# The first expert's order of work: token blocks in halves, the first product's bank copied when its scale is known, weight preparation, maxima and two gate rounds moved

## The chip, the cores and the metric

The kernel runs on one core of a Trainium2 chip. The metric is the device time of one execution in microseconds (us). TensorE (PE) multiplies matrices into PSUM, ACT (ScalarE), DVE (VectorE) and POOL (GpSimd) do the rest, SP issues the DMAs. Each engine works through its own queue in order and waits at an instruction until what it needs is there.

## The reference

Three stages, each feeding the next. Attention over 2 batches, 8 heads, 576 positions and head dimension 64, with a learned bias by relative position. A first mixture: `h = max(x@w1, x@w2, x@w3)`, `x = h@w_out`, on 1152 tokens (512 features, 768 hidden). A second mixture of eight experts:

```python
logits = x @ w_gate
P = np.exp(logits - logits.max())
for _ in range(8):
    P /= P.sum(1, keepdims=True) + 1e-09
    P /= P.sum(0, keepdims=True) + 1e-09
    P *= N / E
for e in range(E):
    h = np.maximum(x @ w1[e], 0.0)
    out += P[:, e:e + 1] * (h @ w2[e])
```

with x of 1152 x 512, `w1[e]` of 512 x 1024 and `w2[e]` of 1024 x 512.

## The kernel before, in words

The change lies at the end of the first mixture and the start of the second. `tc.manual_schedule()` is on: every engine's queue holds its instructions in the order in which the Python code emits them, so the lists of small functions below are the schedule. Numbers are kept as a high and a low half-precision part (`h` and `l` in the names), and each product is three matmuls: high by high, low by high, high by low. A high part is an ACT copy, a low part a subtraction on DVE or GpSimd.

**The last stage of the first mixture** (loop from L1066, matmuls on L1073) makes x in sixteen output tiles, k = 0 to 15, each of 18 matmuls: four feature blocks d for the token groups 0, 2, 1, 3 in this order. After the matmuls of a tile come its eviction (`x_ev`: ACT scales it into `x2f`, DVE takes its maximum into `xm`), and then the steps that `sched[k]` lists. These are:

- `x_top`, `x_scale`: the scale of x.
- `pf0`, `pf1` (from `prep_f`, L930): the weights w1 of the first two halves of the first expert; six steps each: `scale` (ACT into tile `wf`, of which there is one), `s13` and `s24` (two DVE sums each), `a_split` (ACT high, GpSimd low, 768 columns), `hi_s` (ACT, 1024 columns), `lo_s` (GpSimd, 1024 columns).
- `bs0`, `bs1`: the token blocks B11 and B21 for the first and second half of the tokens of a batch (ACT high, GpSimd low).
- `xs0`, and for the second half `last` (both from `x_steps`, L970): the other five token blocks. `t1`, `tb`, `t2`, `t4` are DVE subtractions, `h2` to `h6` high parts on ACT, `l2` to `l6` low parts (`l2` and `g6` on GpSimd, the others on DVE).
- `p2(i)` (`prep_2`, L1025): a quarter of a w2 block: two ACT operations, one GpSimd low part, and the load of a later quarter on SP.
- `pk`, `peak_join`, `peak_send`, `peak_get`, `peak_all`: maxima of raw weights on DVE, sent through memory to all partitions (`SC` is that of w2 of the second block, `S2` of later ones); `b_top` and `b_all` do the same for `SB` on TensorE.

**The second mixture** (loop from L1325) has 32 calls `up(n)` and 16 calls `down(h)`: up(0), up(1), up(2), down(0), up(3), up(4), down(1), up(5) and so on. `up(n)` forms four quarter results with seven products in Strassen's manner (Winograd's form) in three PSUM banks x, z and y; `prod` issues a product of 12 matmuls, `snap` copies a bank on ACT with the scale c, `join` adds a bank on DVE, `relu_hi` (ACT) and `relu_lo` (DVE) write the two parts of h. The first, fourth and sixth products all go into bank x: the fourth can begin only when `snap` has read the first. c comes from the largest |x| (`m_top` and `m_spread`, one small TensorE operation each, then a few DVE operations), and that needs the last tile's maximum. `then(seg)` runs what `between` (and `extra`) put at seven places of an `up`.

`down(h)` runs nine token tiles t of 12 matmuls each into two PSUM banks; each is added into `acc` (ACT for h = 0, DVE after that), and the lists `todo[t]` prepare the next weights. The gate's rounds are spread over this time: `cols` is a small matmul that sums P over the tokens, followed by four DVE operations; `rows` is four DVE operations. In down(0) `rows` stand at t = 0, 2, 4, 6 and `cols` at t = 2, 4, 6; up(4) and up(5) hold two rounds each; up(6) has the last `cols`.

Of the kernel before, what the change touches and what calls it, by code (L numbers as in the profile page):

```python
# [15 lines left out]
ALU = mybir.AluOpType  # L16
# [38 lines left out]
def make_body(stop=None):  # L55
    def body(tc, a):
# [21 lines left out]
        with ctx, tc.manual_schedule():  # L78
# [770 lines left out]
            with ExitStack() as mctx:  # L849
# [120 lines left out]
                def x_steps(s):  # L970
# [6 lines left out]
                    return {"t1": sub(t1, bl(0, 1), bl(0, 0)), "t2": sub(t2, bl(1, 1), t1), "tb": sub(tb, bl(1, 1), bl(0, 1)),  # L977
# [72 lines left out]
                def b_all():  # L1050
# [6 lines left out]
                sched = {0: [x_top], 1: [x_scale], 2: [pf0[0]], 3: pf0[1:3] + [pk(1, 1, 0)], 4: [pf0[3], pk(1, 1, 1)],  # L1057
                         5: [pf0[4], pf0[5], pk(0, 2, 0), pk(0, 2, 1)],
                         6: [bs0[0], pk(0, 2, 2), pk(0, 2, 3), lambda: peak_join(*SB)], 7: [b_top, bs0[1], pf1[0]],
                         8: [b_all] + xs_("t1", "tb", "h2", "l2"), 9: xs_("h3", "h5", "t2") + pf1[1:3], 10: xs_("l3", "l5", "h4") + pf1[3:4],  # L1060
                         11: xs_("l4", "t4") + pf1[4:6] + [pk(1, 2, 0)], 12: xs_("h6", "g6") + [bs1[0], pk(1, 2, 1), pk(1, 2, 2)],
                         13: [bs1[1], p2(0), pk(1, 2, 3), lambda: peak_join(*SC)], 14: [p2(1), lambda: peak_send(SC[0])],
                         15: [end(n) for n in ("t2", "h2", "l2", "h3")]}
                sched[14] += [lambda: last.update(x_steps(1)), end("t1")]
# [31 lines left out]
            with ExitStack() as ectx:  # L1096
# [80 lines left out]
                def m_spread():  # L1177
# [8 lines left out]
                between = {(0, 0): [m_top, end("h4"), end("l3")],  # L1186
                           (0, 1): [m_spread, end("l4"), end("tb"), end("h5"), end("l5")], (0, 2): [end("t4")],
                           (0, 3): [end("h6"), end("l6")], (0, 6): [p2(2)], (1, 5): [p2(3)],
                           (1, 6): [logits], (2, 1): [flip], (2, 2): [gate], (1, 2): [lambda: peak_get(SC[0])],
                           (2, 0): [lambda: peak_all(*SC)], (2, 6): []}  # L1190
# [11 lines left out]
                def up(n, extra):  # L1202
# [11 lines left out]
                    def prod(i, j, bank, start):  # L1214
# [5 lines left out]
                        for c in range(2):  # L1220
                            for ws, xs in ((whi, xth), (whi, xtl), (wlo, xth)):
# [4 lines left out]
                                k += 1  # L1226
                        return ps[bank][:, :, :SH]
# [23 lines left out]
                    then(0)  # L1251
                    z = prod(A12, B21, "z", True)
                    if n == 0:
                        then(1)
                        s1 = snap("s1", x)
# [5 lines left out]
                    if n > 0:  # L1261
                        relu_lo(0, 0, s1)
# [138 lines left out]
```

## Time and profile before

| | us |
|---|---|
| median of three runs | 1076.03 (1075.59 to 1076.33) |
| the profiled execution | 1074.92 |
| its span, first to last instruction | 1073.1 |
| PE busy | 1041.2 (97%) |
| DVE busy | 794.3 (74%) |
| ACT busy | 593.1 (55%) |
| POOL busy | 403.6 (38%) |

The granted clock of TensorE was 0.993 of full speed on average. Times in the rows are from the span's start. Matmuls overlap, and a matmul's end is modelled, so a TensorE that is busy all the time can still lose time; what it loses is read from the spacing of the starts and from the marks of idle time.

### The profile page before, as it was taken

How to read it: one execution, taken by the hardware profiler on the slowest of the kernel's cores; microseconds unless marked ns; L12 is line 12 of the kernel's file. 1: busy time of each engine (PE TensorE's matmuls, PEld its weight loads, DVE VectorE, ACT ScalarE, POOL GpSimd, SP SyncE). 2: the span in 40 equal slices, each digit the busy share in tenths (PEclk: the TensorE clock that was granted, in tenths of full speed). 3: DMA queues.
4: the chain of work that ended last, by engine and by line, in shares of the span. 5: the costliest groups of instructions: out<-in, count | busy, mean ns of one | idle time of the engine just before them, and what ended most of it. 6: DMA issues, size and time to landing. Idle time of an engine off the chain costs nothing.

```text
span 1073.1 us, 18471 instructions
## 1 busy us (share of the span) xinstructions
PE 1041.2 (97%) x7145; PEld 731.8 (68%) x7145; DVE 794.3 (74%) x1547; ACT 593.1 (55%) x1003; POOL 403.6 (38%) x285
## 2 busy tenths in 40 slices
PE   7779999999999899999999999999999999999998
PEld 3259988999999765564755746657566575664753
DVE  8999999799967776877667677566675666757543
ACT  7989988544425666544545444545445454544530
POOL 6996998122214424135132141331413314123120
PEclk8999999999999999999999999999999999999999
DMA  5878764244522012013021120221302203110002
GB/s 187 278 232 276 223 193 136 62 158 118 121 74 84 21 62 64 26 59 84 20 64 36 49 84 21 64 53 32 84 21 65 64 29 76 23 42 6 1 1 89
DMA packets 41063, 90.78 MB, mean 85 GB/s; under 512 B 8264, under 2 KB 11280, under 8 KB 40080
## 3 DMA queue, kind: packets, MB, share of 16 engines
q1 hardware_dynamic: 40832, 89.31, 28.3%
q8 instruction: 56, 0.92, 0.4%
q14 instruction: 31, 0.25, 0.1%
q10 hardware_dynamic: 144, 0.29, 0.1%
HBM read 75.50 MB, written 13.30 MB: 83 GB/s over the span
## 4 chain that ended last, share of the span: by engine, by line
PE 83%; DVE 9%; ACT 3%; POOL 2%; issue 2%; DMA 0%; DVEq 0%; ACTq 0%; POOLq 0%
PE d L1304 34%; PE x L1223 12%; PE m L658 10%; PE y L1223 8%; PE z L1223 8%; PE sc L482 3%; PE o L1073 2%; PE pv L608 2%; POOL s L356 2%; PE pt L556 2%; DVE ng L499 1%; PE p L381 1%; DVE ptl L570 1%; DVE hl L1244 1%; DVE s L1235 1%
## 5 line engine op out<-in xcount | busy, mean ns | idle before, releaser
L1304 PE MATMUL d<-w2h,hl 128*128 128x512 f16 x576 | 218.3, 379 | 0.2 <-DVE hl L1244 0.2
L1304 PE MATMUL d<-w2h,hh 128*128 128x512 f16 x576 | 218.3, 379 | 0.0
L1304 PE MATMUL d<-w2l,hh 128*128 128x512 f16 x576 | 218.3, 379 | 0.0
L1223 PEld LDWEIGHTS <-w1h 128*128 128x128 f16 x1792 | 175.0, 98 | 52.6 <-issue 5.7
L1304 PEld LDWEIGHTS <-hh 128*128 128x128 f16 x1152 | 112.6, 98 | 132.4 <-ACT hh L1239 0.4
L953 POOL TENSOR_TENSOR w1l<-wf,w1h 128x768 f16<-128x768 f32 x32 | 53.2, 1663 | 362.6 <-ACT w1h L952 289.4
L1318 DVE SCALAR_TENSOR_TENSOR acc<-d,kh,acc 128x512 f32<-128x512 f32 x126 | 94.3, 749 | 93.7 <-PE d L1304 93.6
L1239 ACT ACTIVATE hh<-s 128x576 f16<-128x576 f32 x128 | 87.3, 683 | 128.5 <-DVE s L1235 99.9
L1244 DVE SCALAR_TENSOR_TENSOR hl<-s,hh 128x576 f16<-128x576 f32 x128 | 99.2, 776 | 46.7 <-ACT hh L1239 44.2
L959 POOL TENSOR_TENSOR w1l<-wf,w1h 128x1024 f16<-128x1024 f32 x32 | 69.3, 2166 | 117.1 <-ACT w1h L956 117.1
L956 ACT ACTIVATE w1h<-wf 128x1024 f16<-128x1024 f32 x32 | 33.8, 1055 | 131.2 <-DVE wf L949 131.2
L1304 PEld LDWEIGHTS <-hl 128*128 128x128 f16 x576 | 56.4, 98 | 68.5 <-DVE hl L1244 0.7
L1223 PEld LDWEIGHTS <-w1l 128*128 128x128 f16 x896 | 87.7, 98 | 22.1
L1231 ACT ACTIVATE s<-x,cx 128x576 f32<-128x576 f32 x96 | 70.4, 733 | 28.5 <-PE x L1223 28.3
L1223 PE MATMUL x<-xth,w1h 128*128 128x288 f16 x384 | 78.4, 286 | 2.9 <-ACT s L1231 2.9
L1034 POOL TENSOR_TENSOR w2l<-w2r,w2h 128x512 f16<-128x512 f32 x64 | 74.0, 1178 | 17.5 <-ACT w2h L1033 17.5
L1223 PE MATMUL x<-xth,w1l 128*128 128x288 f16 x384 | 78.4, 286 | 0.0
L1223 PE MATMUL x<-xtl,w1h 128*128 128x288 f16 x384 | 78.4, 286 | 0.0
L1235 DVE SCALAR_TENSOR_TENSOR s<-z,cx,s 128x576 f32<-128x576 f32 x64 | 52.3, 818 | 31.3 <-PE z L1223 24.9
L658 PE MATMUL m<-xl,wh 128*128 128x384 f32 x216 | 72.5, 336 | 0.0
L658 PE MATMUL m<-xh,wh 128*128 128x384 f32 x216 | 72.4, 335 | 0.0
L658 PE MATMUL m<-xh,wl 128*128 128x384 f32 x216 | 72.4, 335 | 0.0
(225 smaller groups left out, 2332.7 us busy)
## 6 DMA issues: line engine op xcount, KB each, us to landing
wr<-in_moe_w SPq DMA_DIRECT2D x50, 512.0 KB, 3.6
w2r<-in_moe_w SPq DMA_DIRECT2D x64, 256.0 KB, 2.8
bias_f<-bo SPq DMA_DIRECT2D x36, 295.5 KB, 3.4
bias<-bias_f SPq DMA_DIRECT2D x32, 288.0 KB, 2.8
qk<-in_qk SPq DMA_DIRECT2D x7, 1152.0 KB, 6.9
wr<-in_moe_w_out SPq DMA_DIRECT2D x6, 512.0 KB, 5.3
vr<-in_v SPq DMA_DIRECT2D x8, 320.0 KB, 7.2
bias<-bias_f SPq DMA_DIRECT2D x16, 144.0 KB, 5.0
```

Of the source, the lines that this page charges most:

```text
L658: T.matmul(out=p[:, :TG], lhsT=ws[:, 128 * c:128 * c + 128], rhs=xs[:, c, TG * g:TG * g + TG], start=(c == 0 and n == 0), stop=(c == 3 and ...
L953: G.tensor_tensor(out=lo[:, 0:3], in0=t[:, 1:4], in1=hi[:, 0:3], op=ALU.subtract)
L956: A.activation(out=hi[:, 3:7], in_=t[:, 4:8], func=AF.Copy)
L959: G.tensor_tensor(out=lo[:, 3:7], in0=t[:, 4:8], in1=hi[:, 3:7], op=ALU.subtract)
L1034: G.tensor_tensor(out=lo, in0=r, in1=hi, op=ALU.subtract)
L1223: T.matmul(out=ps[bank][:, s, :SH], lhsT=ws[:, i, c, :], rhs=xs[:, j, c, s * SH:s * SH + SH], start=(start and k == 0), stop=(k == 5), **kw)
L1231: A.activation(out=t, in_=src, func=AF.Identity, scale=c)
L1235: V.scalar_tensor_tensor(out=out, in0=z, scalar=scale, in1=out, op0=ALU.mult, op1=ALU.add)
L1239: A.activation(out=o, in_=src, func=AF.Relu)
L1244: V.scalar_tensor_tensor(out=l, in0=src, scalar=0.0, in1=o, op0=ALU.max, op1=ALU.subtract)
L1304: T.matmul(out=pd, lhsT=hs[:, fh, 128 * t:128 * t + 128], rhs=ws, start=(k == 0), stop=(k == 11))
L1318: V.scalar_tensor_tensor(out=acc[:, t, :], in0=pd, scalar=kh[:, 1 + t:2 + t], in1=acc[:, t, :], op0=ALU.mult, op1=ALU.add)
```

## The change

It splits three steps of block B22 for the second half of the tokens by feature half (`t2a`, `t2b` and so on); reorders `sched`, so that the first token blocks come at k = 4 and 5, the second weight half at k = 6 to 8, the first two `p2` at k = 9 and 10, and the three maxima of `SC` leave k = 11 to 13; gives `prod` a place in the middle (`mid`), at which up(0) now runs `m_top`; puts the copy `s1` of up(0) directly behind `then(1)`, ahead of the copy `s5`, and the join behind `then(2)`; spreads the steps of `last` anew over up(0); takes the four maxima of `SC` into up(2) and its `peak_all` into down(0); and moves the two gate rounds of up(5) into down(1), t = 4 and 5.

```diff
@@ -974,7 +974,16 @@
                     sub = lambda o, x, y: lambda: V.tensor_tensor(out=o, in0=x, in1=y, op=ALU.subtract)
                     hi = lambda i, t: lambda: x_high(i, t, s)
                     lo = lambda i, t, eng=V: lambda: x_low(i, t, s, eng)
-                    return {"t1": sub(t1, bl(0, 1), bl(0, 0)), "t2": sub(t2, bl(1, 1), t1), "tb": sub(tb, bl(1, 1), bl(0, 1)),
+                    def part(n, q):
+                        h = xth[:, 2, q:q + 1, s * SH:s * SH + SH]
+                        b = bl(1, 1)[:, q:q + 1]
+                        return {"t": lambda: V.tensor_tensor(out=t2[:, q:q + 1], in0=b, in1=t1[:, q:q + 1], op=ALU.subtract),
+                                "h": lambda: A.activation(out=h, in_=b, func=AF.Copy),
+                                "l": lambda: G.tensor_tensor(out=xtl[:, 2, q:q + 1, s * SH:s * SH + SH], in0=b, in1=h,
+                                                             op=ALU.subtract)}[n]
+
+                    return {n + "2" + "ab"[q]: part(n, q) for n in "thl" for q in range(2)} | {
+                            "t1": sub(t1, bl(0, 1), bl(0, 0)), "t2": sub(t2, bl(1, 1), t1), "tb": sub(tb, bl(1, 1), bl(0, 1)),
                             "t4": sub(t2, t2, bl(1, 0)), "h2": hi(2, bl(1, 1)), "l2": lo(2, bl(1, 1), G),
                             "h3": hi(3, t1), "l3": lo(3, t1), "h4": hi(4, t2), "l4": lo(4, t2), "h5": hi(5, tb), "l5": lo(5, tb),
                             "h6": hi(6, t2), "l6": lo(6, t2), "g6": lo(6, t2, G)}
@@ -1054,14 +1063,14 @@
                 p2 = lambda i: lambda: prep_2(i)
                 xs_ = lambda *names: [xs0[n] for n in names]
                 end = lambda n: lambda: last[n]()
-                sched = {0: [x_top], 1: [x_scale], 2: [pf0[0]], 3: pf0[1:3] + [pk(1, 1, 0)], 4: [pf0[3], pk(1, 1, 1)],
-                         5: [pf0[4], pf0[5], pk(0, 2, 0), pk(0, 2, 1)],
-                         6: [bs0[0], pk(0, 2, 2), pk(0, 2, 3), lambda: peak_join(*SB)], 7: [b_top, bs0[1], pf1[0]],
-                         8: [b_all] + xs_("t1", "tb", "h2", "l2"), 9: xs_("h3", "h5", "t2") + pf1[1:3], 10: xs_("l3", "l5", "h4") + pf1[3:4],
-                         11: xs_("l4", "t4") + pf1[4:6] + [pk(1, 2, 0)], 12: xs_("h6", "g6") + [bs1[0], pk(1, 2, 1), pk(1, 2, 2)],
-                         13: [bs1[1], p2(0), pk(1, 2, 3), lambda: peak_join(*SC)], 14: [p2(1), lambda: peak_send(SC[0])],
-                         15: [end(n) for n in ("t2", "h2", "l2", "h3")]}
-                sched[14] += [lambda: last.update(x_steps(1)), end("t1")]
+                sched = {0: [x_top], 1: [x_scale], 2: [pf0[0]], 3: pf0[1:3] + [pk(1, 1, 0)],
+                         4: [pf0[3], bs0[0], pk(1, 1, 1)], 5: [pf0[4], pf0[5], bs0[1], pk(0, 2, 0), pk(0, 2, 1)],
+                         6: [pf1[0], pk(0, 2, 2), pk(0, 2, 3), lambda: peak_join(*SB)], 7: [b_top] + pf1[1:4],
+                         8: [b_all] + pf1[4:6] + xs_("t1", "tb", "h2", "l2"), 9: xs_("h3", "h5", "t2") + [p2(0)],
+                         10: xs_("l3", "l5", "h4") + [p2(1)], 11: xs_("l4", "t4"), 12: xs_("h6", "g6") + [bs1[0]],
+                         13: [bs1[1], lambda: last.update(x_steps(1))],
+                         14: [end(n) for n in ("t1", "h3", "l3", "h2a", "l2a", "t2a")],
+                         15: [end(n) for n in ("t2b", "h2b", "l2b", "h4")]}
                 evs = []
                 for n, g in enumerate((0, 2, 1, 3)):
                     for d in range(4):
@@ -1183,11 +1192,12 @@
                     V.tensor_scalar(out=nc_, in0=c, scalar1=-1.0, scalar2=None, op0=ALU.mult)
                     V.tensor_scalar(out=kx, in0=cx[:, 1:2], scalar1=xs[:, 1:2], scalar2=2.0 ** 8, op0=ALU.mult, op1=ALU.mult)
 
-                between = {(0, 0): [m_top, end("h4"), end("l3")],
-                           (0, 1): [m_spread, end("l4"), end("tb"), end("h5"), end("l5")], (0, 2): [end("t4")],
-                           (0, 3): [end("h6"), end("l6")], (0, 6): [p2(2)], (1, 5): [p2(3)],
-                           (1, 6): [logits], (2, 1): [flip], (2, 2): [gate], (1, 2): [lambda: peak_get(SC[0])],
-                           (2, 0): [lambda: peak_all(*SC)], (2, 6): []}
+                between = {(0, 0): [m_top], (0, 1): [m_spread, end("l4"), end("tb"), end("t4")],
+                           (0, 2): [end("h5"), end("l5")], (0, 3): [end("h6")], (0, 4): [end("l6")],
+                           (0, 6): [p2(2)], (1, 5): [p2(3)],
+                           (1, 6): [logits], (2, 1): [flip, pk(1, 2, 0), pk(1, 2, 1)],
+                           (2, 2): [gate, pk(1, 2, 2), pk(1, 2, 3), lambda: peak_join(*SC), lambda: peak_send(SC[0])],
+                           (2, 6): [lambda: peak_get(SC[0])]}
                 kh_t = {}
 
                 def gains(h):
@@ -1211,7 +1221,7 @@
                         for f in between.get((n, seg), []) + extra.get(seg, []):
                             f()
 
-                    def prod(i, j, bank, start):
+                    def prod(i, j, bank, start, mid=None):
 
                         if start:
                             ps[bank] = ps_u.tile([128, 2, 512], F32, tag=bank, name=bank)
@@ -1224,6 +1234,8 @@
                                              rhs=xs[:, j, c, s * SH:s * SH + SH],
                                              start=(start and k == 0), stop=(k == 5), **kw)
                                 k += 1
+                            if mid is not None and k == 3:
+                                then(mid)
                         return ps[bank][:, :, :SH]
 
                     def snap(tag, src):
@@ -1248,24 +1260,26 @@
                     x = prod(A11, B11, "x", True)
                     if n > 0:
                         s1 = snap("s1", x)
-                    then(0)
-                    z = prod(A12, B21, "z", True)
-                    if n == 0:
+                        then(0)
+                        join(s1, prod(A12, B21, "z", True), c)
+                        relu_hi(0, 0, s1)
+                        then(1)
+                        s5 = snap("s5", prod(S1, T1, "y", True))
+                        relu_lo(0, 0, s1)
+                        then(2)
+                        s2 = snap("s2", prod(S2, T2, "x", False))
+                    else:
+                        z = prod(A12, B21, "z", True, mid=0)
                         then(1)
                         s1 = snap("s1", x)
-                    join(s1, z, c)
-                    if n > 0:
-                        relu_hi(0, 0, s1)
-                        then(1)
-                    s5 = snap("s5", prod(S1, T1, "y", True))
-                    if n > 0:
-                        relu_lo(0, 0, s1)
-                    then(2)
-                    s2 = snap("s2", prod(S2, T2, "x", False))
+                        s5 = snap("s5", prod(S1, T1, "y", True))
+                        then(2)
+                        join(s1, z, c)
+                        s2 = snap("s2", prod(S2, T2, "x", False))
+                    then(3)
                     if n == 0:
                         relu_hi(0, 0, s1)
                         relu_lo(0, 0, s1)
-                    then(3)
                     y = prod(S4, B22, "y", False)
                     join(s2, y, c)
                     relu_hi(0, 1, s2)
@@ -1294,6 +1308,11 @@
                             2: [fa[1], lambda: peak_get(S2[0])], 3: [fa[2], fa[3], p2(0)], 4: [fa[4], fa[5], p2(1)],
                             5: [p2(2)], 6: [p2(3), lambda: peak_all(*S2)], 7: [fb[0], fb[1], fb[2], fb[3]],
                             8: [fb[4], fb[5]]}
+                    if h == 0:
+                        todo[2].insert(0, lambda: peak_all(*SC))
+                    if h == 1:
+                        for t in (4, 5):
+                            todo[t] += [lambda: cols(ps_u), rows]
                     for t in range(NTT):
                         pd = ps_d.tile([128, 512], F32, tag="d", name="d")
                         k = 0
@@ -1327,7 +1346,7 @@
                         extra = {}
                         if n == 1:
                             extra = {i: [f] for i, f in enumerate(prep_f(2))}
-                        for seg in {4: (1, 4), 5: (1, 4)}.get(n, ()):
+                        for seg in {4: (1, 4)}.get(n, ()):
                             extra.setdefault(seg, []).extend((lambda: cols(ps_d), rows))
                         if n == 6:
                             extra[1] = [lambda: cols(ps_d)]
```

## Rows read from the trace of the kernel before

**Rows 1.** The page's part 4: shares of the chain that ended last, by engine.

```profile
PE 83%; DVE 9%; ACT 3%; POOL 2%; issue 2%; DMA 0%; DVEq 0%; ACTq 0%; POOLq 0%
```

**Rows 2.** Timeline of PE: start us, us, instruction, [idle before, releaser].

```profile
363.05 0.41 PE L1223 MATMUL x<-xth,w1h 128*128 128x288 f16 x2 [2.34 <-ACT s L1231]
...
389.73 0.40 PE L1223 MATMUL y<-xth,w1h 128*128 128x288 f16 x2
...
476.26 0.41 PE L1223 MATMUL z<-xth,w1h 128*128 128x288 f16 x2 [0.51 <-DVE s L1235]
```

**Rows 3.** Windows: stretch, us, busy (instructions) of PE, PEld, DVE, ACT, POOL, PEclk, DMA.

```profile
355.07:369.62 14.55, 11.32 (x90) 8.46 (x88) 10.99 (x23) 8.23 (x14) 5.30 (x4) 1.00 0.16 38
369.62:380.73 11.11, 10.70 (x84) 8.10 (x84) 7.60 (x13) 8.74 (x13) 2.80 (x2) 1.00 0.23 77
508.56:518.85 10.29, 10.29 (x85) 8.22 (x84) 5.41 (x8) 5.06 (x7) 2.67 (x2) 1.00 0.08 31
```

**Rows 4.** Timeline of DVE, 339 to 387: subtractions of 576 columns.

```profile
339.95 1.08 DVE L974 TENSOR_TENSOR t<-acc 128x576 f32<-128x576 f32 x1
...
348.07 2.60 DVE L974 TENSOR_TENSOR t<-t,acc 128x576 f32<-128x576 f32 x1
...
356.86 0.75 DVE L974 TENSOR_TENSOR t<-acc,t 128x576 f32<-128x576 f32 x1
...
382.97 3.85 DVE L1244 SCALAR_TENSOR_TENSOR hl<-s,hh 128x576 f16<-128x576 f32 x2 [0.16 <-ACT hh L1239]
```

**Rows 5.** Timeline of POOL, beside the second and the last of these.

```profile
347.37 2.68 POOL L959 TENSOR_TENSOR w1l<-wf,w1h 128x1024 f16<-128x1024 f32 x1
...
383.56 2.64 POOL L959 TENSOR_TENSOR w1l<-wf,w1h 128x1024 f16<-128x1024 f32 x1
```

**Rows 6.** Timeline of POOL, 329 to 336.

```profile
329.42 1.67 POOL L953 TENSOR_TENSOR w1l<-wf,w1h 128x768 f16<-128x768 f32 x1 [23.47 <-ACT w1h L952]
...
334.11 1.29 POOL L964 TENSOR_TENSOR xtl<-acc,xth 128x576 f16<-128x576 f32 x1
```

**Rows 7.** Timeline of ACT, the high part of 1024 columns.

```profile
330.87 1.05 ACT L956 ACTIVATE w1h<-wf 128x1024 f16<-128x1024 f32 x1
```

**Rows 8.** Timeline of DVE, from the last maximum to the scale c.

```profile
356.77 0.17 DVE L1087 TENSOR_REDUCE m<-xm 128x1 f32<-128x16 f32 x1
...
359.74 0.15 DVE L1182 TENSOR_SCALAR cx<-cx 128x1 f32<-128x1 f32 x1
```

**Rows 9.** Timeline of DVE in down(0), the round of t = 4.

```profile
408.88 0.91 DVE L1162 SCALAR_TENSOR_TENSOR P<-P,col 128x72 f32<-128x72 f32 x1
...
410.09 1.76 DVE L1152 TENSOR_SCALAR row<-row 128x9 f32<-128x9 f32 x1
...
412.13 0.89 DVE L1154 TENSOR_TENSOR P<-P,row 128x72 f32<-128x72 f32 x1
```

**Rows 10.** Timeline of PE, the column sum of t = 6 in down(0).

```profile
413.17 0.30 PE L1158 MATMUL pc<-P,ones 128*128 128x72 f32 x1
```

**Rows 11.** Timeline of DVE in down(0), the round of t = 2, first and last operation.

```profile
403.19 0.22 DVE L1159 TENSOR_REDUCE col<-pc 128x8 f32<-128x72 f32 x1
...
404.88 0.23 DVE L1154 TENSOR_TENSOR P<-P,row 128x72 f32<-128x72 f32 x1
```

**Rows 12.** Timeline of DVE in down(1), the accumulation of t = 4.

```profile
453.32 0.75 DVE L1315 SCALAR_TENSOR_TENSOR acc<-d,kh,acc 128x512 f32<-128x512 f32 x1 [0.72 <-PE d L1304]
```

**Rows 13.** Timeline of POOL in down(1), from t = 4 on.

```profile
453.77 2.13 POOL L959 TENSOR_TENSOR w1l<-wf,w1h 128x1024 f16<-128x1024 f32 x1 [6.07 <-ACT w1h L956]
455.86 3.39 POOL L1034 TENSOR_TENSOR w2l<-w2r,w2h 128x512 f16<-128x512 f32 x3
```

**Rows 14.** Timeline of PE in down(1), the first matmul of t = 6.

```profile
455.71 0.38 PE L1304 MATMUL d<-w2h,hh 128*128 128x512 f16 x1
```

**Rows 15.** Windows near the start; columns as in rows 3.

```profile
6.80:10.10 3.30, 0.00 (x0) 0.00 (x0) 2.94 (x14) 3.07 (x5) 1.91 (x2) 1.00 0.61 253
10.60:17.20 6.60, 5.77 (x89) 5.02 (x92) 5.80 (x13) 5.50 (x10) 5.27 (x4) 0.50 0.03 8
```

## The prediction, made before the change was run

> **What bounds the kernel now.** The page first: 83% of the chain that ended last is TensorE [rows 1], so only what makes TensorE wait, or adds to its queue, moves the end. Second, TensorE's timeline around the change, for its idle marks: in up(0) it waits 2.34 us for ACT's copy `s1` of the x bank, and in up(6) 0.51 us for a DVE join [rows 2]. The mark counts from a modelled end, 0.41 us after a pair of matmuls begins, where the next pair can begin after 0.245; the loss is 0.17 larger: 2.5 and 0.7. Third, busy time by stretch: an undisturbed `up` of seven products (84 matmuls) takes 10.29 us, so a product 1.47; up(0) took 14.55 and up(1) 11.11 [rows 3]. With 4.2 lost in up(0), 0.8 in up(1), 0.3 in up(2) (y at 389.73 came that much after its turn [rows 2]) and 0.7 at up(6), some 6 us is all that can be won. Fourth, DVE and GpSimd (POOL) side by side. A DVE subtraction of 576 columns from two SBUF tiles takes 0.75 us; the one at 348.07 took 2.60 and ended 0.62 after the GpSimd operation beside it. Of two such in a row at 382.97 (3.85 us for both), the second let a GpSimd operation go ahead that had asked in between [rows 4, 5]. So these operations take turns, each whole. Reductions and operations on one column per partition do not wait.
>
> **First expert, stretches 4 to 15 (k numbers the sixteen output tiles).** I walk the four queues in their new order with the old durations. k=4 and 5: GpSimd gets, after the first `lo` (1.67 us) [rows 6], the low half of a token block (1.29), the second `lo` (2.13 to 2.16) and another token half: 329.42 to about 335.7. `pf1[0]` writes tile `wf`, which that second `lo` reads until 334.45, so ACT's scale of the second block runs 334.5 to 335.7 (before: 336.18). k=7: DVE's four sums (0.34 us each) now meet the GpSimd `lo` of 1.67 that starts with them at 336.9, and end at 339.9, not 338.3. k=8: ACT's `hi` takes 1.05 [rows 7], to 340.98, and GpSimd takes the port at 341.06, while DVE is at its small scalar operations until 341.26. `t1` waits for GpSimd's 2.13 and ends 343.8 (before: 341.03 [rows 4]); GpSimd's token half goes next, and `tb` ends 345.6. ACT, in order, does `h3`, `h5`, `p2(0)`, eviction 10, `h4`, `p2(1)`, evictions 11 and 12: until 350.6. `l4` waits for the GpSimd part of `p2(1)`; `t4` ends 352.3 (before: 350.67). All behind it is 1.7 us late: the low halves of the second token blocks are ready at 355.7 and, after `t1'` has had its turn, 357.4.
>
> The end of it: on DVE `l3'` and `t2a` now stand ahead of the last maximum, and each waits for a GpSimd turn: `l3'` ends 358.0, `t2a` 358.9, the maximum 359.5 (before: 356.94 [rows 8]). TensorE does x with 0.3 us of waiting, half of z with another 0.3, waits for the maximum to 359.6, does the other half, the spread, y. The scale c is there at 361.7 (before: 359.90), the copy `s1` at 362.4, and the fourth product starts at 362.5 instead of 363.05: the early copy is worth 0.6 us here. But behind c the DVE still has `l4'`, `tb'`, `t4'`, `l5'`, a join, a low part, a join and `l6'` (eight of 0.67 to 0.81, and some 1.5 us of waiting for ACT between): `l6'` ends 368.9. It stood ahead of that second join before; now the seventh product waits for it from its fourth matmul, and up(1) starts at 370.1, not 369.62: 0.45 lost. If no operation met another at the port, c would come at 359.2 and up(1) start at 367.4 (2.2 won); with every turn lost, 370.3. I take my walk.
>
> up(1): `s3` and the join of up(0) are then done before TensorE asks, and ACT reaches `s5` earlier against TensorE: of the 0.8 lost 0.65 is won (0 to 0.8). up(2): `peak_all` (0.85 us) leaves the head of DVE's queue, so the join that held `s5` comes 0.8 earlier and y waits no more: 0.3 won. The four maxima put in there (0.67 each, and 0.16) fill DVE's idle time in up(2); DVE leaves it 0.35 us later against TensorE than before. That costs nothing at once, since down(0) reads the blocks of up(0) and up(1). First expert together: 0.5 us won (bounds: 0.5 lost, 3.1 won).
>
> **down(0).** DVE gets `peak_all` for the second block at t=2. The round that begins at t=4 had no slack: its last operation ended 413.02, and TensorE's next column sum stood at 413.17 in its queue, 0.15 after that end [rows 9, 10]. What is put ahead, 0.85, and the 0.35 that DVE is late, are paid: 1.2 us lost. Bounds: 0.3, if DVE's last sum of t=3 still asks for the port before the GpSimd `lo` of 406.94; 1.65, if it asks after it. The peaks' trip through memory, sent at 391 and fetched in 6 to 8 us, is over well before 405.
>
> **down(1): two gate rounds.** A round is four DVE operations from the column sum (L1159 on) and four for the rows. Free of GpSimd it takes 403.19 to 405.11, 1.9 us; beside GpSimd its slow ones were L1162 (0.91 us), L1152 (1.76) and L1154 (0.89 instead of 0.23), and from L1162's begin alone to the end 408.88 to 413.02 went by, 4.1 us [rows 9, 11]; L1160 can wait as well. In down(0) and up(4) a column sum stands every 5.3 or 4.5 us. In down(1) it stands at t=4 and at t=5, one tile or 2.6 us apart, and TensorE's queue is in order: the second cannot start before the first round has ended, and four tiles wait behind it. Before, DVE's accumulation of t=4 runs 453.32 to 454.07, GpSimd's operations 453.77 to 455.90 and, three in a row, 455.86 to 459.25 [rows 12, 13]. The round begins at 454.0 and meets exactly these: L1160 ends 455.93, L1162 457.1, L1152 458.2, L1154 459.33. With the 0.15 from DVE to TensorE seen at 413.02 to 413.17, and 0.17 for the sum, the tile that started at 455.71 [rows 14] starts at 459.6: 3.9 us lost. Bounds: without any turn the round ends at 456.0 and 0.5 is lost; if DVE is as late there as it leaves up(2), 4.3. I take 3.9: the row nearest to it is the same code beside the same GpSimd operations.
>
> On the port the Trainium skill, "SBUF — State Buffer" (SBUF: two separate sides), says that VectorE and GpSimd hold a shared pair of ports for a whole instruction, and the other is blocked. By that the rounds cost what I sum; if the two only shared bandwidth, nine elements would not take 1.76 us, and down(1) would lose 0.5. The trace agrees with the page (L1152) [rows 9].
>
> **up(5) and up(6).** Two rounds leave up(5); there the second kept DVE 1.9 us ahead of the join for which z of up(6) waits. z's wait of 0.7 [rows 2] goes: 0.7 won (0.4 to 0.7). The column sums themselves, 0.11 to 0.17 of TensorE each, only move.
>
> **At nothing:** halving `t2'`, `h2'`, `l2'` adds three short operations, already in the walk. `p2(0)`, `p2(1)` go from k=13 and 14 to 9 and 10 and issue their two loads on SP some 7 us earlier, where SP has nothing else; the load behind the scale of `pf1` moves by 1.6 us. Uncovered, each would cost a DMA that down(1) needs 80 us later, so nothing.
>
> **Sum.** −0.5 + 1.2 + 3.9 − 0.7 = +3.9 us. The profiled execution took 1074.92 (span 1073.1), so 1078.8 for one like it; it was 1.1 below the median of the three runs, 1076.03, and I give the time on that median: 1079.9.
>
> **Rivals.** (A) The forecast: slower by 3.9, own range +2.2 to +5.5; chance 0.5. (B) The walk of k=7 to 15 is too dark, and c comes at 359.2: 3.1 won instead of 0.5, the stalls stay; +1.3, 1077.3. For it: the turn that makes `t1` late is lost by only 0.2 us, 341.06 against 341.26; if `t1` asks first, the chain behind it is 2 us earlier. Against: GpSimd's asking hangs on the same DVE sum as DVE's own, so both shift together. Or a stall half as long, about as much. Chance 0.25. (C) The other side: the waits at the port do not appear at the new places, since GpSimd's queue shifts against DVE's. Then the first expert wins 3.1, down(0) loses 0.3, down(1) 0.5, up(6) wins 0.7: −3.0, 1073.0. It decides in down(1): the round must end by 456, for which GpSimd's three operations must begin after it; the trace has them at 455.86. Chance 0.13. (D) The clock. TensorE stood idle for 3.3 us at 6.8 us, and then had a granted clock of 0.50 for 6.6 us, that is 1.2 GHz instead of 2.4 [rows 15]; after the 2.34 us at 360.7 it kept 1.00 [rows 3]. The stall in down(1) is longer than either. A fall of that length would cost half of 6.6 us, 3.3, and one of half the length 1.6: 1081.5 to 1083.2, chance 0.1. The Trainium skill, "TensorE: Matmul & The Clock Gate" (What's actually happening), has the clock go back to 1.2 GHz after an idle time; the start of this trace agrees. The last 0.02 is left to a loss above that.
>
> **How the numbers follow.** The likeliest is 1079.9. The range 1074.6 to 1082.3 takes in B and the forecast's bounds; outside it stay C and the upper part of D, and a little at each edge. The forecast's own range is 1078.2 to 1081.5. Within 0.2%, which is what a measurement of this kernel tells from no change, is 1073.9 to 1078.2. Faster: C, 0.13. Same: B, and the edge of A, 0.26. Slower: the rest of A, D and what is above, 0.61.
>
> **What would show it.** In the changed trace: `t1` of the first half longer than 2 us; the last maximum after 358.5; TensorE's wait at the fourth product gone or below 0.5, and a new one in the seventh; a wait of over 1 us before the third column sum of down(0); one of 2.5 to 4 us before the second column sum of down(1), with the four slow DVE operations beside GpSimd; no wait at z of up(6). Wrong would be: in the changed kernel, up(1) starting within 13 us of up(0), or the second sum of down(1) following its tile without idle time.

## The result, and the profile after

| | before | after |
|---|---|---|
| median | 1076.18 us (1074.9 to 1077.62, 6 runs) | 1082.10 us (1080.26 to 1083.66, 6 runs) |
| the profiled execution, its span | 1074.92, 1073.1 | 1083.66, 1081.9 |

The ratio after to before is 1.0054, with the 95% interval 1.0043 to 1.0065: the change costs 5.8 us (4.6 to 7.0). The forecast was 3.9.

The page's part 4 of the kernel after, shares of the chain that ended last (before: [rows 1]):

```profile
PE 78%; DVE 13%; ACT 4%; issue 2%; POOL 2%; DMA 1%; DVEq 0%; ACTq 0%; SPq 0%; POOLq 0%
```

VectorE's share went from 9 to 13%: TensorE waits for it at more places. Where, the lengths of the blocks tell, each taken from the start of its first matmul to that of the next block's (up(1): to the end of its own products, since the gate's logits follow), in one profiled execution of each kernel; in the profiled executions of the experiments, blocks that no edit touches repeat to some 0.05 us where the clock is the same.

| block | before | after | difference | forecast |
|---|---|---|---|---|
| up(0) | 14.54 | 15.22 | +0.68 | +0.45 |
| up(1) | 11.11 | 10.70 | −0.41 | −0.65 |
| up(2) | 11.86 | 11.57 | −0.29 | −0.3 |
| down(0) | 23.95 | 25.49 | +1.54 | +1.2 |
| up(3) | 10.64 | 10.99 | +0.35 | 0 |
| up(4) | 10.84 | 10.64 | −0.20 | 0 |
| down(1) | 23.40 | 29.08 | +5.68 | +3.9 |
| up(5) | 10.64 | 10.29 | −0.35 | 0 |
| up(6) | 11.13 | 10.46 | −0.67 | −0.7 |

The differences add up to +6.3. The later blocks are equal, but for up(24), 0.2 longer. From the start of up(0) to the end it is 718.0 us before and 724.5 after. The stretch ahead of up(0) was 2.2 us longer in the profile after. All of that lies in its first 200 us, ahead of everything that the change touches: from the first mixture's first matmul on, 157.4 us go by to up(0) in both, and the last stage, whose side steps were reordered, takes 40.1 in both. The first 200 us vary by that much between the executions profiled here, which is why blocks are compared, and not spans.

Windows, columns as in [rows 3]: of the kernel before, down(0) and down(1); of the kernel after, up(0), down(0), down(1), and a stretch inside down(1).

```profile
394.65:418.60 23.95, 23.95 (x115) 11.29 (x115) 19.20 (x55) 16.30 (x24) 8.32 (x6) 1.00 0.24 71
440.08:463.48 23.40, 23.40 (x111) 10.56 (x108) 18.15 (x37) 11.27 (x15) 9.33 (x7) 1.00 0.27 84
```

```profile
357.32:372.54 15.22, 11.79 (x89) 8.45 (x88) 12.00 (x25) 7.89 (x14) 4.56 (x4) 1.00 0.02 2
396.87:422.36 25.49, 24.16 (x116) 11.29 (x116) 22.41 (x60) 16.12 (x24) 8.46 (x6) 1.00 0.26 70
443.98:473.06 29.08, 25.66 (x114) 11.46 (x112) 24.68 (x53) 11.27 (x15) 9.32 (x7) 0.94 0.29 68
464.00:467.40 3.40, 3.40 (x9) 1.22 (x8) 1.49 (x8) 0.00 (x0) 0.00 (x0) 0.50 0.37 124
```

After the change down(1) has a mean granted clock of 0.94; the last line holds what makes it so: 3.4 us at 0.50, that is 1.2 GHz.

The timeline of PE in the kernel after, where up(0) waits (before: [rows 2]), where down(0)'s third column sum stands (before: [rows 10]), and down(1) from its second sum on:

```profile
362.00 0.27 PE L1183 MATMUL pmx<-ident,m 128*1 128x128 f32 x1 [1.65 <-DVE m L1096]
...
364.96 0.40 PE L1233 MATMUL x<-xth,w1h 128*128 128x288 f16 x2
...
371.44 0.28 PE L1233 MATMUL z<-xtl,w1h 128*128 128x288 f16 x1 [1.33 <-DVE xtl L964]
...
416.93 0.41 PE L1167 MATMUL pc<-P,ones 128*128 128x72 f32 x2 [1.33 <-DVE P L1163]
...
463.36 0.41 PE L1167 MATMUL pc<-P,ones 128*128 128x72 f32 x2 [3.42 <-DVE P L1163]
463.61 0.38 PE L1323 MATMUL d<-w2h,hh 128*128 128x512 f16 x1
463.82 0.45 PE L1323 MATMUL d<-w2l,hh 128*128 128x512 f16 x1
464.07 0.63 PE L1323 MATMUL d<-w2h,hl 128*128 128x512 f16 x1
464.49 0.63 PE L1323 MATMUL d<-w2h,hh 128*128 128x512 f16 x1
...
467.45 0.38 PE L1323 MATMUL d<-w2l,hh 128*128 128x512 f16 x1
467.67 0.38 PE L1323 MATMUL d<-w2h,hl 128*128 128x512 f16 x1
```

The fourth product's wait of 2.34 us is gone (its first pair, at 364.96, carries no mark), and two others stand in its place, at the transpose for the last maximum and in the seventh product. The second sum of down(1) waits 3.42 by its mark, 3.6 by the spacing of the starts. Behind it the starts are 0.43 us apart instead of 0.215, from 464.07 to 467.45.

What the sum waited for: the timeline of DVE and that of POOL in the kernel after, the round of t = 4 in down(1).

```profile
457.21 0.75 DVE L1334 SCALAR_TENSOR_TENSOR acc<-d,kh,acc 128x512 f32<-128x512 f32 x1 [0.72 <-PE d L1323]
457.88 0.22 DVE L1168 TENSOR_REDUCE col<-pc 128x8 f32<-128x72 f32 x1
458.14 1.68 DVE L1169 TENSOR_SCALAR col<-col 128x8 f32<-128x8 f32 x1
459.85 0.20 DVE L1170 RECIPROCAL col<-col 128x8 f32<-128x8 f32 x1
460.09 0.90 DVE L1171 SCALAR_TENSOR_TENSOR P<-P,col 128x72 f32<-128x72 f32 x1
461.02 0.23 DVE L1160 TENSOR_REDUCE row<-P 128x9 f32<-128x72 f32 x1
461.29 0.76 DVE L1161 TENSOR_SCALAR row<-row 128x9 f32<-128x9 f32 x1
462.08 0.21 DVE L1162 RECIPROCAL row<-row 128x9 f32<-128x9 f32 x1
462.33 0.88 DVE L1163 TENSOR_TENSOR P<-P,row 128x72 f32<-128x72 f32 x1
```

```profile
457.66 2.13 POOL L959 TENSOR_TENSOR w1l<-wf,w1h 128x1024 f16<-128x1024 f32 x1 [6.06 <-ACT w1h L956]
459.74 3.38 POOL L1043 TENSOR_TENSOR w2l<-w2r,w2h 128x512 f16<-128x512 f32 x3
```

Four operations of DVE that take about 0.2 us alone end at 459.82, 460.99, 462.05 and 463.21, each just behind the end of one of GpSimd's four (the first at 459.79, the last at 463.12). That is DVE and GpSimd taking turns, each operation whole; "the port" below is short for that. The round takes 5.33 us; the forecast's walk had 454.0 to 459.33, the same length.

### The profile page after: what moved, and what is told of

Its sections match the earlier page's. It is cut to its first block, busy times and chain, and to the rows that moved or that the text cites. A ratio compares the mean times of both kernels' runs of the same rounds, so it can differ in the third digit from the quotient of the medians.

```text
span 1081.9 us, 18478 instructions
## 1 busy us (share of the span) xinstructions
PE 1041.8 (96%) x7145; PEld 730.0 (67%) x7145; DVE 802.2 (74%) x1548; ACT 593.7 (55%) x1004; POOL 404.1 (37%) x286
## 4 chain that ended last, share of the span: by engine, by line
PE 78%; DVE 13%; ACT 4%; issue 2%; POOL 2%; DMA 1%; DVEq 0%; ACTq 0%; SPq 0%; POOLq 0%
PE d L1323 32%; PE x L1233 11%; PE m L658 10%; PE y L1233 8%; PE z L1233 8%; PE sc L482 2%; PE pv L608 2%; PE pt L556 2%; DVE ng L499 1%; DVE ptl L570 1%; POOL s L356 1%; PE o L1082 1%; DVE bo L400 1%; DMA bias<-bias_f 1%; DVE hl L1256 1%
```

## The experiments

Each was timed against the kernel before; ratios are to it, with the 95% interval. Windows have the columns of [rows 3].

**e1_rounds_back and e2_rounds_only: the change in two halves.** e1 is the kernel after with the two rounds back in up(5); e2 is the kernel before with only that move.

```
e1, on after:   -  if h == 1: for t in (4, 5): todo[t] += [cols, rows]
                -  for seg in {4: (1, 4)}      +  for seg in {4: (1, 4), 5: (1, 4)}
e2, on before:  the same two edits the other way round
```

> The changed kernel with the two gate rounds back in up(5). My theory: the second round of down(1) costs 3.7 us of waiting and 1.7 us of half clock behind it, and its leaving up(5) gave back 1.0. Then down(1) takes 23.4 us again instead of 29.1, z of up(6) waits 0.7 again, and the kernel is 4.7 us faster than the changed one, that is within 2 us of the one before (ratio to it 1.000 to 1.003). Rival, that the first expert's new order carries the loss: it stays 4 us or more above the one before.

> The kernel before with nothing but the two rounds of up(5) moved to t = 4 and 5 of down(1). My theory: the second column sum of down(1) waits 3.6 to 3.9 us as in the changed kernel, with or without a fall of the clock behind it; 2.7 to 4.7 us slower than before (1.0025 to 1.0045). Rival, that the wait needs what the first expert's order does to DVE: below 1 us slower.

e1: 1.0012 (1.0002 to 1.0022). e2: 1.0048 (1.0035 to 1.0060), somewhat more than the 1.0025 to 1.0045 expected. In e1 down(1) is 23.40 again, up(5) 10.64 and up(6) 11.14, and the rest is as in the kernel after. In e2 down(1) is 28.91. Window of down(1) in e1; then, of e2, that of down(1) and of its clock's fall, and those of up(0) and of a fall there:

```profile
443.15:466.55 23.40, 23.40 (x110) 10.56 (x108) 18.15 (x37) 11.27 (x15) 9.33 (x7) 1.00 0.35 84
```

```profile
442.75:471.67 28.92, 25.50 (x115) 11.56 (x113) 24.76 (x53) 11.27 (x15) 9.32 (x7) 0.94 0.28 67
461.80:465.20 3.40, 3.07 (x9) 1.44 (x10) 2.54 (x10) 0.00 (x0) 0.10 (x1) 0.50 0.57 157
357.29:372.79 15.50, 12.81 (x90) 9.24 (x89) 11.46 (x23) 8.20 (x14) 5.27 (x4) 0.89 0.15 36
366.20:369.60 3.40, 3.40 (x17) 2.15 (x15) 1.40 (x3) 1.88 (x3) 0.00 (x0) 0.50 0.06 5
```

The move of the rounds alone is nearly the whole loss, 5.2 of 5.8 us (in e2's profiled execution down(1), up(5) and up(6) make +4.5 of it), and the rest of the change costs 1.3 us (0.2 to 2.4), where the forecast's terms for it were −0.5 + 1.2. The last two lines are a surprise: behind up(0)'s old wait of 2.5 us, which the kernel before had with a clock of 1.00 [rows 3], the clock fell in this execution.

**e3_filled: the clock apart from the wait.** The kernel after, with sixteen more matmuls, whose result nobody reads, in TensorE's queue ahead of the second sum of down(1). They lie inside the wait.

```
+  def fill(): w = ps_u.tile(...); 16 x T.matmul(out=w[:, i % 2, :], lhsT=hts[0][0][:, 0, 0:128], rhs=w2t[h, 0, 0][0])
   todo[4] += [cols, rows]
-  todo[5] += [cols, rows]      +  todo[5] += [fill, cols, rows]
```

> The changed kernel with 16 matmuls of 512 columns, read by nobody, ahead of the second column sum of down(1): 3.5 us of TensorE work in the wait of 3.6. Theory, that the idle time dropped the clock: the sum starts at the same time after its tile (3.6 to 3.8 us), the granted clock stays at 1.00 behind it, down(1) takes 27.4 us instead of 29.1; 1 to 1.7 us faster than the changed kernel. Rival, that the slow stretch behind the wait has another cause: down(1) stays at 29 or takes longer.

Measured 1.0047 (1.0034 to 1.0059). Windows of down(1), of up(0), and of a fall in up(0):

```profile
442.99:470.40 27.41, 27.41 (x130) 12.56 (x128) 24.70 (x53) 11.27 (x15) 9.33 (x7) 1.00 0.27 70
355.02:371.56 16.54, 13.25 (x90) 9.23 (x88) 11.99 (x25) 7.78 (x13) 4.53 (x4) 0.90 0.02 2
360.70:364.10 3.40, 3.40 (x15) 2.27 (x16) 2.85 (x10) 0.74 (x1) 0.00 (x0) 0.50 0.00 0
```

With TensorE busy through the wait, down(1) keeps 1.00 and is 1.67 us shorter, with the same round ahead of its second sum: the 5.68 is 4.0 of waiting and sums and 1.7 of clock. The time as a whole does not show it: 1 to 1.7 us less than the kernel after were expected, it is 0.8 less, and the intervals of the two ratios overlap. In the profiled execution the clock fell in up(0) instead, which was then 1.3 longer; whether the other timed executions fell there too is not shown.

That the idle time brought the clock down rests on three profiled executions: it fell behind the wait in the kernel after and in e2, and did not behind the filled wait of e3. The mean granted clock, on record for every timed execution, points the same way, loosely. One fall of 3.41 us takes 0.0016 off it (half of 3.41 in 1080). None of the eleven executions of the kernel after and e2, which have the wait, is above 0.995; four of the sixteen of e1 and e4, which do not, are. The means are 0.9935 (after), 0.9924 (e2), 0.9942 (e3), 0.9943 (e1) and 0.9954 (e4), and single executions of one of these kernels lie up to 0.004 apart.

**e4_lows_on_dve: the wait without its cause.** The kernel after, with the four low parts that GpSimd computes in down(1) from t = 4 on given to DVE, behind the second round; the loads that follow three of them move with them.

```
-  G.tensor_tensor(out=lo, in0=r, in1=hi, op=ALU.subtract)        (p2(1) to p2(3), and lo_s of up(5)'s weights)
+  V.tensor_tensor(out=lo, in0=r, in1=hi, op=ALU.subtract)        (issued in todo[5] behind cols, rows, and in todo[6])
```

> The changed kernel, in which the four GpSimd low parts that meet the rounds of down(1) are done by DVE behind the second round. Theory, that the two engines take turns at a port: the first round takes 1.95 us instead of 5.3, the second column sum waits 0.4 to 0.8 us instead of 3.6, the clock does not fall, and the kernel is 4.5 to 5 us faster than the changed one. Rival, that eight dependent DVE operations and the accumulation are too long for one tile by themselves: the wait stays above 2 us.

Measured 1.0035 (1.0022 to 1.0048). DVE in the same round (its operations from the second on), and the windows of down(1) and up(5):

```profile
457.62 0.17 DVE L1179 TENSOR_SCALAR col<-col 128x8 f32<-128x8 f32 x1
457.83 0.20 DVE L1180 RECIPROCAL col<-col 128x8 f32<-128x8 f32 x1
458.06 0.23 DVE L1181 SCALAR_TENSOR_TENSOR P<-P,col 128x72 f32<-128x72 f32 x1
...
459.05 0.23 DVE L1173 TENSOR_TENSOR P<-P,row 128x72 f32<-128x72 f32 x1
```

```profile
443.46:467.69 24.23, 24.14 (x114) 10.99 (x112) 22.46 (x54) 10.34 (x14) 2.76 (x2) 1.00 0.27 66
467.69:479.08 11.39, 10.61 (x85) 8.21 (x84) 7.02 (x10) 5.87 (x9) 3.77 (x2) 1.00 0.17 57
```

The same eight operations, 1.68 + 0.90 + 0.76 + 0.88 us for the slow four beside GpSimd, take 0.17 + 0.23 + 0.17 + 0.23 here; the round is 1.9 us long, the second sum waits 0.2, down(1) falls from 29.08 to 24.23. So GpSimd's four operations beside the round were the cause of the wait, and eight DVE operations alone are not too long for a tile. DVE, which now has the low parts too, is late in up(5) and gives 1.1 us back there. The kernel was expected 4.5 to 5 us below the kernel after: from the start of up(0) to the end the profiled executions differ by 3.8 (720.7 against 724.5), the times by 2.0 only, with intervals that just leave room for 3.8. The Trainium skill, "SBUF — State Buffer" (SBUF: two separate sides), calls the pair of ports that VectorE and GpSimd share an exclusive lock for the whole instruction; that the four end with GpSimd's four, and are short without them, agrees.

**e5_max_first, e6_t1_first, e7_peaks_later, e8_three: the three smaller waits.** All stand on e1. e5 puts the last maximum ahead of the four DVE and ACT steps `l3'`, `t2a`, `t2b`, `h4'`; e6 puts the copies and differences of the first token half ahead of the last two steps of the second weight block; e7 puts down(0)'s `peak_all` for the second block from t=2 to t=3, behind all four DVE sums of up(3)'s weights; e8 is all three.

```
e5:  -  14: [t1, h3, l3, h2a, l2a, t2a], 15: [t2b, h2b, l2b, h4]     (0, 0): [m_top]
     +  14: [t1], 15: [h3, h2a, l2a, h2b, l2b]                       (0, 0): [m_top, l3, t2a, t2b, h4]
e6:  -  8: [b_all] + pf1[4:6] + xs_("t1", "tb", "h2", "l2"), 9: xs_("h3", "h5", "t2") + ...
     +  8: [b_all] + xs_("t1", "tb", "h2", "l2"), 9: xs_("h3", "h5") + pf1[4:6] + xs_("t2") + ...
e7:  -  todo[2].insert(0, peak_all(*SC))      +  todo[3].insert(1, peak_all(*SC))
```

> The changed kernel with the rounds back in up(5), and with l3', t2a', t2b' and h4' of the second token half moved behind the last maximum (into up(0), behind m_top); h3' behind the last eviction. My theory: in the changed kernel the last maximum is late because two waits for GpSimd's turn stand ahead of it on DVE; now it ends about 2.7 us earlier against the start of up(0) (4.5 us before), the wait in z falls from 1.65 to below 0.3, and up(0) takes 13.2 to 13.8 us instead of 15.2. Rival, that up(0) is set by DVE's work behind the scale c alone: up(0) stays above 14.8.

> The changed kernel with the rounds back in up(5), and at k = 8 and 9 with t1, tb, h2, l2, h3, h5 ahead of the last two weight steps of pf1. Theory, that t1 of the first half is late because GpSimd's lo_s takes the port 0.2 us before it: t1 takes 0.75 us instead of 2.60, the low half of the second token block is ready 1 to 1.5 us earlier against the start of up(0), the waits in its first two products (0.37 and 0.29) go, and up(0) takes 13.9 to 14.6 us. Rival, that the shared port is full over the whole stretch, so that the turn is only lost elsewhere: up(0) stays within 0.4 of 15.2.

> The changed kernel with the rounds back in up(5), and with peak_all of the second block behind the two DVE sums of t = 3 of down(0) instead of ahead of those of t = 2. Theory, that the 1.5 us lost in down(0) come from DVE's second pair of sums asking for the port after GpSimd's lo: the pair ends ahead of it, the third column sum of down(0) waits less than 0.4 us instead of 1.5, down(0) takes 23.9 to 24.3 us instead of 25.5, and the kernel is 1.2 to 1.6 us faster than with the rounds back alone. Rival, that the 0.85 us of DVE work cost what they cost wherever they stand before that round: down(0) stays at 24.8 or more.

> All three edits on the kernel with the rounds back in up(5): maximum first, t1 first, peaks later. If they add, up(0) takes 12.2 to 13.2 us (14.5 before), down(0) 24, and the time from the start of up(0) to the end is 715 to 717 us against 718.0 before, so 1 to 3 us faster than before (ratio 0.997 to 0.999). Rival, that DVE's chain behind the scale sets up(0): up(0) not below 13.5, no faster than before.

| | ratio | up(0) | down(0) | up(3) |
|---|---|---|---|---|
| e1 | 1.0012 (1.0002 to 1.0022) | 15.20 | 25.51 | 10.97 |
| e5 | 1.0003 (0.9994 to 1.0011) | 14.29 | 25.50 | 10.99 |
| e6 | 1.0001 (0.9992 to 1.0010) | 13.90 | 25.49 | 10.99 |
| e7 | 1.0010 (1.0001 to 1.0020) | 15.19 | 23.93 | 12.09 |
| e8 | 0.9997 (0.9988 to 1.0006) | 13.55 | 23.93 | 12.10 |

Each wait goes where its cause is taken away, and each time a later one takes a part of it. In e5 the transpose no longer waits, but the fourth product does, 1.1 us for `s1`, and up(0) misses the 13.2 to 13.8 expected. In e6 the waits in the first two products go, and up(0) is at the lower end of what was expected. In e7 down(0) came as expected, so its 1.5 us were the lost turn and not `peak_all` as such; but the 1.6 won there come back as 1.1 lost in up(3), and the time is 0.2 us below e1's, not 1.2 to 1.6. Timelines of ACT and DVE in e7, where that is:

```profile
420.31 1.15 ACT L940 ACTIVATE wf<-wr,pw 128x1024 f32<-128x1024 f32 x1 [1.34 <-DVE pm L773]
...
424.42 1.06 ACT L956 ACTIVATE w1h<-wf 128x1024 f16<-128x1024 f32 x1 [1.51 <-DVE wf L949]
425.39 0.72 ACT L1243 ACTIVATE s<-x,cx 128x576 f32<-128x576 f32 x1
```

```profile
422.62 1.77 DVE L949 TENSOR_TENSOR wf<-wf 128x256 f32<-128x256 f32 x1
```

The scale waited for maxima that stand on DVE behind the round of t = 6, L949 lost its turn at the port (as it does in the kernel after, 1.77 too), and the snapshot `s1` of up(3) stands behind all of it on ACT. e8's expected 0.997 to 0.999 was missed for this reason, and since its fourth and seventh products still wait 1.0 and 1.5. Its up(0) of 13.55 and its ratio are what its rival said.

**e9_l6_early to e12_one_round: the waits that were left, one after the other.** Each has the edits of the one before it, e9 those of e8.

```
e9:   -  (0, 2): [h5, l5], (0, 3): [h6], (0, 4): [l6]         +  (0, 2): [h5, h6, l5, l6]
e10:  -  z = prod(A12, B21, "z", True, mid=0); then(1)        +  then(0); z = prod(A12, B21, "z", True, mid=1)
e11:  peak_all(*S2) of down(0) from todo[6] to todo[5]
e12:  -  5: (1, 4)      +  5: (1,)      and in down(1):  +  todo[6] += [cols, rows]
```

> The three moves of e8_three, and on top the last low part of the x bank (its copy and its subtraction) one product earlier. Theory (the seventh product of up(0) waits 1.6 us only because this subtraction stands on VectorE behind the work that the scale c released): the wait at the third matmul of the seventh product goes, up(0) falls from 13.55 to 12.0 to 12.2 us, first expert's start to end from 717.8 to 716.3, ratio to before 0.998. Rival (the wait moves to the next reader, since VectorE has the same work in sum): up(0) 12.0 but up(1) longer by 0.5 to 1.5, ratio 0.9990 or more.

> e9_l6_early, and the two small matmuls of the last maximum half a product earlier each. Theory (c sets the fourth product's wait of 1.0 us): c comes 0.4 to 0.8 us earlier, the wait falls to 0.2 to 0.5, up(0) 11.3 to 11.8 us, ratio 0.9975. Rival (the fourth product then waits for the x bank's copy h4 and its low part, since the same subtractions on VectorE come first): up(0) 12.0 or more, as in e9_l6_early.

> e10_top_early, and in down(0) the maxima that up(4)'s weights need one token block earlier, ahead of the round of t = 6 that takes turns with GpSimd. Theory (up(3) waits for its first snapshot because the scaling of the weights on ScalarE waited for these maxima, 1.3 us): up(3) 12.1 to 10.7 to 11.0 us, down(0) unchanged at 23.9, ratio 0.9963. Rival (VectorE and GpSimd take turns on the four weight operations whenever these start): up(3) 11.7 or more, or down(0) up by 0.3 or more.

> e11_peaks_t5, and one of up(5)'s two gate rounds in down(1) at t = 6, where no second column sum follows it closely. Theory (the change's down(1) lost its 5.7 us to the second sum behind the first round, not to the move as such): down(1) 23.5 to 23.7 us, clock 1.00 there, up(5) 10.4 to 10.6, up(6) 10.5 to 10.8, ratio 0.9960. Rival (any round beside GpSimd's low parts delays what follows): down(1) 24.5 us or more, or up(5) over 11, ratio at or above e11_peaks_t5's.

| | median, us | ratio | up(0) + up(1) | up(3) | down(1) | up(5) + up(6) |
|---|---|---|---|---|---|---|
| e8 | 1075.93 | 0.9997 (0.9988 to 1.0006) | 24.26 | 12.10 | 23.40 | 21.77 |
| e9 | 1075.67 | 0.9992 (0.9983 to 1.0001) | 24.37 | 12.08 | 23.40 | 21.77 |
| e10 | 1074.92 | 0.9984 (0.9976 to 0.9993) | 24.24 | 12.08 | 23.39 | 21.77 |
| e11 | 1074.06 | 0.9978 (0.9969 to 0.9987) | 24.22 | 10.64 | 23.39 | 21.77 |
| e12 | 1073.23 | 0.9975 (0.9965 to 0.9986) | 24.23 | 10.64 | 23.56 | 20.92 |

PE's waits in e9, and windows of up(3) in e11 and of down(1), up(5) and up(6) in e12:

```profile
362.59 0.41 PE L1233 MATMUL x<-xth,w1h 128*128 128x288 f16 x2 [0.86 <-ACT s L1243]
...
369.88 0.41 PE L1233 MATMUL x<-xth,w1h 128*128 128x288 f16 x2 [1.05 <-ACT s L1243]
```

```profile
417.19:427.82 10.63, 10.45 (x85) 8.21 (x84) 5.71 (x8) 5.84 (x9) 3.77 (x2) 1.00 0.19 57
```

```profile
440.69:464.26 23.57, 23.57 (x113) 10.79 (x111) 18.59 (x43) 11.27 (x15) 9.52 (x7) 1.00 0.36 85
464.26:474.72 10.46, 10.46 (x87) 8.42 (x86) 7.81 (x18) 5.05 (x7) 2.50 (x2) 1.00 0.06 25
474.72:485.19 10.47, 10.47 (x89) 8.42 (x87) 7.29 (x16) 5.51 (x8) 5.48 (x7) 1.00 0.01 2
```

e9's theory failed and its rival held: the 1.5 us left the seventh product, and now the first of up(1) waits 1.2 and the second 0.3. The first needs the snapshot `s3`, on ACT behind a chain of joins on DVE that c releases. e10 cut the fourth product's wait by 0.2 us only, to 0.8, and both blocks together by 0.13, near its rival; its ratio is better by more than that, 0.0008, with intervals that overlap. e11's theory held for the blocks: up(3) 10.64, a little better than expected, and down(0) unchanged. e12's blocks came as expected too: one of the two rounds at t = 6 costs down(1) 0.17 and gives up(5) and up(6) 0.85. The times missed: 0.9975, 0.9963 and 0.9960 were expected of e10 to e12.

What made e12's round cheap is not told apart. It has no second sum close behind it, as its theory says, but it does not stand beside GpSimd's operations either, so its rival was not put to the test. GpSimd and DVE around the round in e12, its first and last operation:

```profile
456.46 3.40 POOL L1043 TENSOR_TENSOR w2l<-w2r,w2h 128x512 f16<-128x512 f32 x3
462.99 1.65 POOL L953 TENSOR_TENSOR w1l<-wf,w1h 128x768 f16<-128x768 f32 x1 [3.13 <-issue]
```

```profile
461.10 0.22 DVE L1168 TENSOR_REDUCE col<-pc 128x8 f32<-128x72 f32 x1
...
462.79 0.23 DVE L1163 TENSOR_TENSOR P<-P,row 128x72 f32<-128x72 f32 x1
```

GpSimd is idle from 459.86 to 462.99, and the round takes 1.9 us, as it does alone. e12 beats the kernel before by 0.25% (0.14 to 0.35), and is 8.9 us below the median after.

## Why the prediction was right, and where its size was off

**The sign and the main mechanism were right.** TensorE waits for DVE, DVE for its turn at the port, at the places forecast. With 2.24 us, by which up(0) began later, added to the forecast's times: `t1` took 2.60 us, the last maximum ended 361.86 against 361.7, c was there at 364.07 against 363.9, the fourth product no longer waits, the seventh does, up(1) starts at 372.54 against 372.3. up(0)'s +0.45 became +0.68: the 0.2 is there already at the fourth product, 364.96 against 364.7.

**The size came out within the range, but not by the forecast.** 5.8 us lie above the forecast's own bounds of +2.2 to +5.5, and 1082.10 lies 0.2 below the top of the whole range; without the fall of the clock, to which the sum gave nothing, the time would have been some 1080.4 by estimate (1082.1 − 1.7), if the clock fell in the timed executions as in the profiled one. The blocks lost 6.3 where the forecast had 3.9. Of the 2.4 between, down(1) is 1.8, up(0) to up(2) together 0.5 (nothing won instead of 0.5), down(0) and up(3) 0.35 each; up(4) and up(5) take 0.55 off.

**down(1) is the term that was mis-sized: 3.9 forecast, 5.68 measured.** The round itself was forecast to 0.01 us. What the term lacked is the clock: behind the wait of 3.6 us TensorE ran 3.41 us at 1.2 GHz, which costs half of it, 1.7 us. That is rival D, there with a chance of 0.1 and a price of 1.6 for a fall of this length; it came on top of A. The argument against it was that the clock had stayed at 1.00 after 2.34 us [rows 2, 3]; but a wait that had not led to a fall said little of one half as long again. In both executions profiled with the wait of 3.6 (after, e2) the clock fell; in the one with TensorE busy in the same place (e3) it did not.

**down(0): 1.2 forecast, 1.54 measured**, near the upper bound of 1.65 that was named for a lost turn; the forecast's 1.2 lay between its two bounds. Timelines of DVE and of POOL in the kernel after:

```profile
409.33 1.84 DVE L949 TENSOR_TENSOR wf<-wf 128x256 f32<-128x256 f32 x1
```

```profile
409.24 1.64 POOL L953 TENSOR_TENSOR w1l<-wf,w1h 128x768 f16<-128x768 f32 x1 [20.53 <-issue]
```

GpSimd was 0.09 us ahead, and the last of DVE's sums took 1.84 instead of 0.42.

**up(3): 0 forecast, +0.35 measured.** This step was missing: DVE leaves down(0) 0.6 us later against TensorE, ACT begins the scale of up(4)'s weights 0.3 later behind it, and the fifth product of up(3) waits 0.7 instead of 0.36 for an ACT copy (marks 0.54 and 0.19, and 0.17 each). **up(4) −0.20 and up(5) −0.35** were not forecast. The former is a wait of the second product that is gone. The latter is the two column sums, 0.17 each (10.64 with two, 10.46 with one in e12, 10.29 with none); they only move, as the prediction said, and are in down(1)'s 5.68. **up(6)** came as forecast.

**Rival B** (the first expert better than the walk) is refuted by the blocks up(0) to up(2), which together win nothing, and by e1: without the rounds the change still costs 1.3 us. **Rival C** (no turns lost) is refuted by the round of 5.33 us; e4 shows what it would have looked like.

**What stays open**: what decides whether the clock falls behind a wait of 1.7 to 2.5 us (below), how often it falls behind the 3.6, why e4's time fell by less than its blocks, and what e10 won outside the blocks it touched.

## What to carry to other kernels

When a small chain of DVE operations is moved, price it by what GpSimd does at the new place, operation by operation, and not by its own duration: eight operations took 1.9 us alone and 5.3 beside four of GpSimd. Where a matmul in an in-order queue waits for such a chain, two copies in consecutive tiles stall the engine for all that the first is late. With room behind it even a chain beside GpSimd can cost next to nothing (the kernel before, down(0): the sum stood 0.15 us behind the round's end [rows 9, 10]), and e12's, with room behind and GpSimd idle, cost 0.17 us, its column sum. A stall longer than any that the profile has seen at full clock is to be priced with the clock's fall too, here half as much again. Waits taken away one by one tend to reappear at the next reader: e7 gave back 1.1 of 1.6 us until the next maxima were moved too (e11).

## What the runs showed of the hardware that was not expected

A wait of the same length does not always bring the clock down. With the 2.5 us ahead of the fourth product it fell in e2 and not in the kernel before; with the 1.7 us at the transpose and smaller waits ahead of it, it fell in e3 and not in after, e1, e4 and e7. Each fall seen after the first 20 us and ahead of the last matmuls lasted 3.41 us at 1.2 GHz. Starts of 512 columns were then 0.43 us apart instead of 0.215; the Trainium skill, "TensorE: Matmul & The Clock Gate" (Wait — 56ns, not 53.3ns?), gives 426.7 ns at 1.2 GHz and 215.7 at 2.4, and the trace agrees.
